# Turning batch 3's k with the transposing DMA in place of TensorE, and loading batch 4's k one slot sooner, in a sliding-window attention and MLP kernel

## The chip, the core and the metric

The kernel runs on one core of a Trainium2 chip. Its engines are TensorE (PE in the profile; PEld are its weight loads), VectorE (DVE), ScalarE (ACT), GpSimd (POOL) and SyncE (SP, which here does nothing but issue DMAs in order). Each engine works through its own queue in order and waits for the others by semaphores. The metric is the device time of one execution in microseconds.

## The reference

Attention with 8 batches, 8 heads, 576 positions and a head size of 64, in float32; a position sees itself and the 127 before it, and a bias that falls with the distance is added. The result, with the heads side by side, goes through a two-layer MLP with a hard-swish between the layers.

```python
scores = scale * np.matmul(q, k.transpose(0, 1, 3, 2))
bias = slopes[:, None, None] * (-np.abs(rel).astype(np.float32))[None, :, :]
mask = (rel >= 0) & (rel < window)              # window = 128
scores = np.where(mask, scores + bias[None], -1000000000.0)
attn = softmax(scores)                          # written out in the reference
attn_out = np.matmul(attn, v)
x = attn_out.transpose(0, 2, 1, 3).reshape(B * S, H * D)     # 4608 x 512
h = x @ w_in                                    # 512 -> 2048
g = h * np.clip(h + 3.0, 0.0, 6.0) / 6.0
out = g @ w_out                                 # 2048 -> 512
```

## The kernel before

The unit of attention is a pair of heads of one batch, numbered g = 4 x batch + pair, so g runs from 0 to 31. The MLP works on tiles of 512 tokens: 16 groups of matmuls up (`moe_up`, line 513) and 16 down (`moe_down`, line 539) per tile. `fill(n)` (line 574) issues the next n groups of that list, so that TensorE has MLP work between the steps of attention. The order of every queue is the order in which the program is written (`manual_schedule`); nothing reorders it.

From g = 8 on the work runs in `segment` (line 718), one slot per g. A slot has the scores of g (`scores`, lines 365 and 373), its exponentials on ACT (`exp_diag`, `exp_off`, lines 389, 413 and 418), which POOL masks (`affine_select`, lines 406, 415 and 421), and the product with v of the pair before (`values(g - 1, ...)`, lines 434 and 442), which VectorE divides by the row sums (lines 452 and 453). Groups of four MLP matmuls (lines 502 and 552) stand between these steps; an up group is followed by line 521 on ACT and line 522 on VectorE, and each finished block of 128 output rows is copied by VectorE (line 561) and stored by SP (line 562). `back` brings the attention result into the layout of the MLP: for most g by a transposing DMA on SP (line 476), for g = 10 and 11 by TensorE (line 483).

The scores need q and k with the head dimension on the partitions, in `qTb` and `kTb`, two buffers each that batches take in turn. Three ways lead there:

- `transposes`, for batch 0, and `prepare_double` (line 224) with `double` or `wide_double` for batches 1 and 2 and for batch 3's k: the load puts nine positions of each of four heads on one partition, POOL casts to bf16 (line 228), TensorE turns nine blocks of 128x128 (line 243) into PSUM, and ACT or VectorE copies them into `qTb` or `kTb` (line 245). One call of `double` does five or four of the nine blocks. It borrows the PSUM bank "av", which `values` also uses, or "h", which the up groups use.
- For batch 3's q and everything from batch 4 on: `load_tokens` (line 108, five DMAs of 256 KB and less on SP), POOL's cast into the one buffer `tbuf` (`cast_tokens`, line 195) and one transposing DMA of 20 blocks of 128x128 from `tbuf` into `qTb` or `kTb` (`xbar`, line 200). As there is one `tbuf`, POOL can't cast k before the transpose of q has landed.

`stage_next(g)` (line 591), near the end of each slot, issues the loads that the table `LOADS` (line 586) names for the slot, the casts and the transposing DMAs. The float32 loads share four buffers `ldbuf`; batch 4's k goes where batch 3's q was. At most eight DMAs of SP's have a semaphore each, taken in turn.

In the slots that matter here SP's queue reads: slot 9, loads of v3 and the transpose of q3; slot 10, a store, back(9), loads of q4; slots 11 and 12, three stores, loads of k4, the transpose of q4; slot 13, back(12), loads of v4, the transpose of k4. In slots 10 and 11 TensorE turns batch 3's k (`double(3, 0, "k", ...)` and `double(3, 1, "k", ...)`, first half after the scores, second half after the first group of the slot).

Of the kernel before, what the change touches and what calls it, by code (L numbers as in the profile page):

```python
# [11 lines left out]
BF16 = mybir.dt.bfloat16  # L12
# [6 lines left out]
def kernel(  # L19
# [9 lines left out]
    nc = tc.nc  # L29
# [6 lines left out]
    NP = H // 2  # L36
# [200 lines left out]
    def double(b, dp, nm, part, tag, copy):  # L237
        src = st[b, dp, nm]
        t0, t1 = ((0, 5), (5, RT))[part]
        tp = BANKS[tag].tile([128, t1 - t0, 128], BF16, tag=tag, name="tp2",  # L240
                             padded_shape=[128, 8, 128])
        for t in range(t0, t1):
            nc.tensor.transpose(tp[:, t - t0, :], src[:, t, :], ident)  # L243
        dst = (qTb if nm == "q" else kTb)[b % 2][:, 2 * dp:2 * dp + 2, :, :]
        copy(out=dst.rearrange("p i j c -> p i (j c)")[:, :, 0:S].rearrange(  # L245
                 "p i (a t) -> p i a t", t=RT)[:, :, :, t0:t1],
             in_=tp.rearrange("p t (a i) -> p i a t", i=2))

    def wide_double(b, dp, nm, copy):
# [324 lines left out]
    def fill(n):  # L574
        for _ in range(n):
# [3 lines left out]
            if fn is moe_up and done[0] < NP * (min((nt * NT + NT - 1) // S, B - 1) + 1):  # L579
# [3 lines left out]

    V, P, A = nc.vector.tensor_copy, nc.gpsimd.tensor_copy, nc.scalar.copy

    LOADS = {9: "v3", 10: "q4", 12: "k4", 13: "v4", 14: "q5", 16: "k5", 17: "v5", 18: "q6",
             20: "k6", 21: "v6", 22: "q7", 24: "k7", 25: "v7"}

    VCAST = {15: 4, 19: 5, 23: 6, 27: 7}
# [1 line left out]
    def stage_next(g):  # L591
        b, hp = divmod(g, NP)
        nb = b + 1
        if g == 2 * NP:
            cast_tokens(2, "v")
        for n in LOADS.get(g, "").split():
            load_tokens(int(n[1]), n[0])
        if nb == 3 and hp < 2:
            prepare_double(3, hp, (P,), "k")
        if nb == 3 and hp == 1:  # L600
            cast_tokens(3, "q")
            xbar(3, "q")
        elif nb < B and nb > 3 and hp < 2:
            cast_tokens(nb, "qk"[hp])
            xbar(nb, "qk"[hp])
        if VCAST.get(g):
            cast_tokens(VCAST[g], "v")
# [110 lines left out]
    def segment(lo, hi, fills):  # L718
        for g in range(lo, hi + 1):
            f = fills(g)  # L720
            if by_xbar(g - 2):
                done[0] = g - 1
            if lo < g < hi and g != 3 * NP + 1:
                scores(g)
            turn = {2 * NP: (2, 1, "k"), 2 * NP + 1: (2, 1, "q"),
                    2 * NP + 2: (3, 0, "k"), 2 * NP + 3: (3, 1, "k")}.get(g)
            if turn:
                double(*turn, 0, "av", A)
            fill(f[0])
            if turn:  # L730
                double(*turn, 1, *(("h", V) if turn[0] == 2 else ("av", A)))
            if g < hi:
                exp_diag(g, 0)
            fill(f[1])
            if g < hi:
                exp_diag(g, 1)
            if g == 3 * NP:
                cast_tokens(3, "v")
            if g > lo:
                values(g - 1, (0, 1, 2))  # L740
            fill(f[2])
            if g < hi:
                exp_off(g, 0)
            fill(f[3])
            if g < hi:
                exp_off(g, 1)
            if g > lo:
                values(g - 1, (3, 4))
            fill(f[4])
            if g > lo and by_xbar(g - 1):  # L750
                back(g - 1)
            fill(f[5])
            if g < hi:
                stage_next(g)
            fill(1)
            if g == 3 * NP:
                scores(g + 1)
            if g > lo and not by_xbar(g - 1):
                back(g - 1)
                done[0] = g  # L760
            fill(f[6] - 1)
# [51 lines left out]
```

## Time and profile before

| What | Value |
|---|---|
| median of 3 runs | 321.79 us (320.87 to 321.81) |
| profiled execution | 320.94 us, its span 319.2 us |
| granted TensorE clock | 0.999 |
| TensorE busy | 310.1 us (97%) |
| VectorE, ACT, POOL busy | 173.1, 195.7, 141.2 us |
| DMAs | 51.90 MB, 131425 packets |
| L243 transposes on TensorE (batches 2 and 3) | 45, 219 ns each |
| L245 copies on ACT, kTb | 0.73 to 0.77 us each |
| L476 transposing DMAs, 5 blocks | 22, hold SP 1.25 us (median), land in 2.7 |
| L200 transposing DMAs, 20 blocks | 9, hold SP 3.7 to 4.6 us, land 5.3 to 7.4 after issue |

A row of a timeline gives the start, the time taken, the engine, the line of the kernel, the operation and what it writes and reads; in brackets the engine's idle time before it and who ended that. For SP the time is how long the issue held the queue; the data land later. Matmuls are pipelined: four matmuls of 512 columns take 0.87 us from start to start, though the row says 1.03.

### The profile page before, as it was taken

How to read it: one execution, taken by the hardware profiler on the slowest of the kernel's cores; microseconds unless marked ns; L12 is line 12 of the kernel's file. 1: busy time of each engine (PE TensorE's matmuls, PEld its weight loads, DVE VectorE, ACT ScalarE, POOL GpSimd, SP SyncE). 2: the span in 40 equal slices, each digit the busy share in tenths (PEclk: the TensorE clock that was granted, in tenths of full speed). 3: DMA queues.
4: the chain of work that ended last, by engine and by line, in shares of the span. 5: the costliest groups of instructions: out<-in, count | busy, mean ns of one | idle time of the engine just before them, and what ended most of it. 6: DMA issues, size and time to landing. Idle time of an engine off the chain costs nothing.

```text
span 319.2 us, 7124 instructions
## 1 busy us (share of the span) xinstructions
PE 310.1 (97%) x2775; PEld 164.9 (52%) x2775; DVE 173.1 (54%) x338; ACT 195.7 (61%) x334; POOL 141.2 (44%) x249
## 2 busy tenths in 40 slices
PE   7879999999999999999999999999999999999996
PEld 5565465455545454445677654444444444444443
DVE  6667675554355655655565556555656455455510
ACT  4748976877767776676676667666764344244401
POOL 8464493684496477266744673663331000000000
PEclk9999999999999999999999999999999999999999
DMA  7999999999999999998999999962212110000112
GB/s 281 199 323 225 256 260 195 249 231 194 215 252 157 239 208 211 205 222 194 207 205 211 209 190 196 225 93 68 38 39 88 53 36 33 33 33 35 66 56 75
DMA packets 131425, 51.90 MB, mean 163 GB/s; under 512 B 118976, under 2 KB 123328, under 8 KB 131392
## 3 DMA queue, kind: packets, MB, share of 16 engines
q1 hardware_dynamic: 126160, 45.36, 68.0%
q0 software_dynamic: 4224, 4.19, 8.2%
q10 hardware_dynamic: 1008, 1.90, 1.6%
q8 instruction: 21, 0.34, 0.5%
q14 instruction: 12, 0.10, 0.1%
HBM read 36.70 MB, written 9.44 MB: 145 GB/s over the span
## 4 chain that ended last, share of the span: by engine, by line
PE 86%; DMA 5%; ACT 4%; POOL 2%; DVE 2%; issue 1%; POOLq 0%
PE ops L552 38%; PE hps L502 36%; DMA w_in_sb<-in_moe_w_in_dram 3%; PE sce L365 3%; PE av L442 2%; PE av L434 2%; DMA ldbuf<-in_k_dram 2%; ACT r L521 2%; PE ops L533 1%; ACT kTb L245 1%; ACT gbuf L399 1%; PE tp L243 1%; DVE gbuf L522 0%; ACT gbuf L377 0%; PE tb L483 0%
## 5 line engine op out<-in xcount | busy, mean ns | idle before, releaser
L522 DVE SCALAR_TENSOR_TENSOR gbuf<-r,hps 128x512 bf16<-128x512 f32 x144 | 98.7, 688 | 101.0 <-ACT r L521 99.8
L521 ACT ACTIVATE r<-hps,bias 128x512 f32<-128x512 f32 x144 | 98.9, 689 | 86.8 <-PE hps L502 86.6
L502 PE MATMUL hps<-xT,w_in_sb 128*128 128x512 bf16 (+1 forms) x640 | 144.9, 358 | 0.6 <-ACT xT L489 0.3
L552 PE MATMUL ops<-w_out_sb,gbuf 128*128 128x512 bf16 x560 | 137.8, 379 | 0.0
L502 PEld LDWEIGHTS <-w_in_sb 128*128 128x128 bf16 x640 | 59.3, 98 | 55.0 <-issue 0.8
L552 PEld LDWEIGHTS <-gbuf 128*128 128x128 bf16 x560 | 51.9, 98 | 56.3
L415 POOL TENSOR_SCALAR_AFFINE_SELECT po<-po 128x512 bf16<-128x512 bf16 x48 | 30.3, 636 | 32.5 <-ACT po L413 32.4
L406 POOL TENSOR_SCALAR_AFFINE_SELECT pd<-pd 128x512 bf16<-128x512 bf16 x48 | 29.8, 634 | 33.5 <-ACT pd L389 33.5
L389 ACT ACTIVATE pd<-sce,bias_d 128x512 bf16<-128x512 f32 x48 | 31.7, 684 | 5.4 <-PE sce L373 2.7
L561 DVE COPY osb<-ops 128x512 f32<-128x512 f32 x33 | 22.7, 688 | 20.0 <-PE ops L552 17.5
L195 POOL CAST tbuf<-ldbuf 128x512 bf16<-128x512 f32 (+1 forms) x45 | 25.6, 614 | 16.8 <-issue 9.3
L413 ACT ACTIVATE po<-sce,bias_o 128x512 bf16<-128x512 f32 x48 | 33.0, 687 | 0.0
L453 DVE TENSOR_TENSOR avs<-av,rc 128x384 bf16<-128x384 f32 (+1 forms) x48 | 23.6, 491 | 1.6
L442 PEld LDWEIGHTS <-pd 128*128 128x128 bf16 x192 | 14.3, 97 | 8.3 <-issue 0.5
L434 PE MATMUL av<-vbuf,po 128*128 128x65 bf16 x192 | 18.0, 193 | 0.0
L442 PE MATMUL av<-vbuf,pd 128*128 128x65 bf16 x192 | 17.3, 193 | 0.3 <-ACT kTb L245 0.3
L434 PEld LDWEIGHTS <-po 128*128 128x128 bf16 x192 | 14.3, 98 | 2.9 <-DVE avs L453 0.5
L188 POOL CAST vbuf<-ldbuf 128x1024 bf16<-128x1024 f32 x14 | 14.2, 1043 | 3.5 <-DMA ldbuf<-in_v_dram 3.5
L418 ACT ACTIVATE p4buf<-sce,bias_d 128x64 bf16<-128x64 f32 x48 | 15.5, 323 | 0.0
L228 POOL CAST pr<-ldbuf 128x576 bf16<-128x576 f32 x20 | 12.9, 670 | 5.1 <-DMA ldbuf<-in_k_dram 3.1
L365 PE MATMUL sce<-qTb,kTb 64*64 64x192 bf16 (+1 forms) x368 | 11.9, 245 | 0.0
L365 PEld LDWEIGHTS <-kTb 64*64 64x64 bf16 x368 | 7.1, 106 | 8.6 <-issue 8.5
(104 smaller groups left out, 208.4 us busy)
## 6 DMA issues: line engine op xcount, KB each, us to landing
out_dram<-osb SPq DMA_DIRECT2D x33, 256.0 KB, 2.5
ldbuf<-in_v_dram SPq DMA_DIRECT2D x32, 256.0 KB, 5.2
ldbuf<-in_q_dram SPq DMA_DIRECT2D x20, 256.0 KB, 5.3
ldbuf<-in_k_dram SPq DMA_DIRECT2D x16, 256.0 KB, 4.4
ldbuf<-in_q_dram SPq DMA_DIRECT2D x12, 288.0 KB, 7.0
ldbuf<-in_k_dram SPq DMA_DIRECT2D x12, 288.0 KB, 6.3
w_in_sb<-in_moe_w_in_dram POOLq DMA_DIRECT2D x4, 512.0 KB, 9.2
w_out_sb<-in_moe_w_out_dram POOLq DMA_DIRECT2D x4, 512.0 KB, 10.3
```

What stands on the lines that cost most here:

```text
L195: nc.gpsimd.tensor_copy(out=tbuf[:m, :, j, :], in_=s[:m, j, :, :].rearrange("p (i e) d -> p i (e d)", e=2))
L365: nc.tensor.matmul(sce[e][lo:lo + 64, j, :, :].rearrange("p s c -> p (s c)")[:, ds(lo, n)], lhsT=kT[r, j, lo:lo + 64], rhs=qT[r, ds(128 * ...
L389: nc.scalar.activation(out=pd[:, e, :, :], in_=st["sce"][e][:, :, 0, :], func=ACT.Exp, bias=bias_d[:, h:h + 1], scale=scale)
L406: nc.gpsimd.affine_select(out=pd[:, e, :, :], in_=pd[:, e, :, :], pattern=[[0, 4], [1, 128]], channel_multiplier=-1, base=0, compare_op=AL ...
L413: nc.scalar.activation(out=po[:, e, :, :], in_=sc[:, :, 1, :], func=ACT.Exp, bias=bias_o[:, h:h + 1], scale=scale)
L415: nc.gpsimd.affine_select(out=po[:, e, :, :], in_=po[:, e, :, :], pattern=[[0, 4], [-1, 128]], channel_multiplier=1, base=-1, compare_op=A ...
L434: nc.tensor.matmul(out_av, lhsT=po[:, e, qt % 4 if full(g) else qt - 1, :], rhs=vb[:, qt - 1, h, :], start=True, stop=False)
L442: nc.tensor.matmul(out_av, lhsT=d, rhs=vb[:, qt, h, :], start=(qt == 0), stop=True)
L502: nc.tensor.matmul(hps[:, lo:hi], lhsT=w_in_sb[:, ks, ts(ms, 128)], rhs=xT[:, ks, ds(src, hi - lo)], start=(ks == 0), stop=(ks == n_ks - 1))
L521: nc.scalar.activation(out=r6, in_=hps, func=ACT.Relu, bias=bias3[:, 0:1], scale=1.0 / 6.0)
L522: nc.vector.scalar_tensor_tensor(out=gts[nt][:, ms, :], in0=r6, scalar=1.0, in1=hps, op0=ALU.min, op1=ALU.mult)
L552: nc.tensor.matmul(ops[nt, sub], lhsT=gts[nt][:, ms, ts(sub, 128)], rhs=w_out_sb[:, ms, :], start=(ms == 0), stop=(ms == n_ms - 1))
```

## The change

Batch 3's k is no longer turned by `double` on TensorE. Once POOL has cast its halves into `pr` tiles (as before, in slots 8 and 9), a new function `turn_double` issues one transposing DMA of nine blocks on SP for each half, into a second SBUF tile: for the first half in slot 9, behind the loads of v3 and ahead of the transpose of q3, for the second in slot 10, behind the loads of q4. A second new function, `copy_double`, has VectorE copy each turned half into `kTb`, the first late in slot 11 (behind the second part of `values(10)`), the second in slot 13 (behind the first exponential). Four ACT copies out of PSUM go with the 18 transposes, and the "av" bank is no longer borrowed there. In `LOADS`, batch 4's k moves from slot 12 to slot 11, which on SP puts its five loads ahead of the store of slot 12.

```diff
+    def turn_double(b, dp, nm):
+        src = st.pop((b, dp, nm))
+        tp = st[b, dp, nm] = prs.tile([128, RT, 2 * D], BF16, tag="prq", name="pt2")
+        nc.sync.dma_start_transpose(out=tp, in_=src.rearrange("p t c -> p (t c)"))
+
+    def copy_double(b, dp, nm, copy):
+        tp = st.pop((b, dp, nm))
+        dst = (qTb if nm == "q" else kTb)[b % 2][:, 2 * dp:2 * dp + 2, :, :]
+        copy(out=dst.rearrange("p i j c -> p i (j c)")[:, :, 0:S].rearrange(
+                 "p i (a t) -> p i a t", t=RT),
+             in_=tp.rearrange("p t (a i) -> p i a t", i=2))
...
-    LOADS = {9: "v3", 10: "q4", 12: "k4", 13: "v4", 14: "q5", 16: "k5", 17: "v5", 18: "q6",
+    LOADS = {9: "v3", 10: "q4", 11: "k4", 13: "v4", 14: "q5", 16: "k5", 17: "v5", 18: "q6",
...
             load_tokens(int(n[1]), n[0])
+        if nb == 3 and hp in (1, 2):
+            turn_double(3, hp - 1, "k")
         if nb == 3 and hp < 2:
             prepare_double(3, hp, (P,), "k")
...
-            turn = {2 * NP: (2, 1, "k"), 2 * NP + 1: (2, 1, "q"),
-                    2 * NP + 2: (3, 0, "k"), 2 * NP + 3: (3, 1, "k")}.get(g)
+            turn = {2 * NP: (2, 1, "k"), 2 * NP + 1: (2, 1, "q")}.get(g)
             if turn:
                 double(*turn, 0, "av", A)
             fill(f[0])
             if turn:
-                double(*turn, 1, *(("h", V) if turn[0] == 2 else ("av", A)))
+                double(*turn, 1, "h", V)
             if g < hi:
                 exp_diag(g, 0)
+            if g == 3 * NP + 1:
+                copy_double(3, 1, "k", V)
...
             fill(f[4])
+            if g == 2 * NP + 3:
+                copy_double(3, 0, "k", V)
```

## The prediction

> **What bounds the kernel now.** I read the page first (shares, the chain that ended last), then the timelines of TensorE, of the SP queue and of POOL over 68 to 140 us. The page says that TensorE bounds the whole:
>
> ```profile
> span 319.2 us, 7124 instructions
> PE 310.1 (97%) x2775; PEld 164.9 (52%) x2775; DVE 173.1 (54%) x338; ACT 195.7 (61%) x334; POOL 141.2 (44%) x249
> DMA  7999999999999999998999999962212110000112
> PE 86%; DMA 5%; ACT 4%; POOL 2%; DVE 2%; issue 1%; POOLq 0%
> ```
>
> The reader should see two things: TensorE has about 9 us of idle time in all, and the DMA engines are as full as it is until about 208 us (26 slices of 8 us). So a microsecond taken from TensorE is worth one only if its data then also come a microsecond sooner. The timeline of TensorE in slot 10 shows what the change takes away:
>
> ```profile
> 68.80 0.52 PE L365 MATMUL sce<-qTb,kTb 64*64 64x192 bf16 x16
> 69.28 0.45 PE L243 MATMUL tp<-ident,pr 128*128 128x128 bf16 x5
> 69.56 1.03 PE L502 MATMUL hps<-xT,w_in_sb 128*128 128x512 bf16 x4
> 70.58 0.38 PE L243 MATMUL tp<-ident,pr 128*128 128x128 bf16 x4
> 70.80 1.03 PE L552 MATMUL ops<-w_out_sb,gbuf 128*128 128x512 bf16 x4
> 71.99 0.22 PE L442 MATMUL av<-vbuf,pd 128*128 128x65 bf16 x2 [0.17 <-ACT kTb L245]
> ```
>
> The timeline of the SP queue shows what it adds to (second column: how long the issue held the queue):
>
> ```profile
> 70.46 5.51 SPq L112 DMA_DIRECT2D ldbuf<-in_v_dram  x5
> 76.08 3.81 SPq L200 DMA_TRANSPOSE qTb<-tbuf  x1
> 80.40 0.38 SPq L562 DMA_DIRECT2D out_dram<-osb  x1
> 80.88 1.26 SPq L476 DMA_TRANSPOSE xT<-avs  x1
> 82.20 4.50 SPq L112 DMA_DIRECT2D ldbuf<-in_q_dram  x5
> ...
> 89.67 0.33 SPq L562 DMA_DIRECT2D out_dram<-osb  x1
> 90.06 4.50 SPq L112 DMA_DIRECT2D ldbuf<-in_k_dram  x5
> 94.77 3.85 SPq L200 DMA_TRANSPOSE qTb<-tbuf  x1
> ...
> 105.82 3.83 SPq L200 DMA_TRANSPOSE kTb<-tbuf  x1
> ...
> 125.83 3.75 SPq L200 DMA_TRANSPOSE qTb<-tbuf  x1
> ```
>
> Each row begins about 0.1 us after the one before it ends (0.5 once, at 80.40). Between 76 and 126 us the only real pause is 1.8 us ahead of 89.67 (the wait list: that store waited for VectorE). The queue is full. And its transposes end at TensorE, as POOL's and TensorE's timelines show:
>
> ```profile
> 133.43 2.84 POOL L195 CAST tbuf<-ldbuf 128x512 bf16<-128x512 f32 x5 [5.73 <-DMA qTb<-tbuf]
> 137.41 1.22 POOL L415 TENSOR_SCALAR_AFFINE_SELECT po<-po 128x512 bf16<-128x512 bf16 x2
> 138.82 0.23 PE L442 MATMUL av<-vbuf,pd 128*128 128x65 bf16 x2
> ```
>
> **What is removed.** 18 transposes, 4 ACT copies (0.73 to 0.76 us each) and their hand-over of the av bank. Slot 10 (scores at 68.80 to scores at 76.94) lasts 8.14 us and slot 14 (98.16 to 105.33), with the same scores, values and seven groups of four MLP matmuls, 7.17: 0.97 us for nine transposes. Slot 11 (76.94 to 85.37) lasts 8.43, of which back(10) takes 0.38: 8.05 against 7.17, 0.88 us. TensorE gains 0.97 + 0.88 = 1.85 us. The ACT copies lie beside other work and give nothing more.
>
> **What is added on SP.** Two transposes of nine blocks, which the trace lacks. Five blocks (L476) hold the queue 1.25 us and twenty (L200) 3.81: 0.17 per block and 0.4 fixed, so 1.94 us for nine, 2.04 with the usual 0.1 gap. Ends: 1.25 and 3.85. I take 1.94, as the two rows span it. Landing: twenty blocks land 5.3 to 7.4 us after issue, and 2.1 us behind the load ahead of them (k4's last landed 4.5 after 93.47, the transpose of q4 5.3 after 94.77): 0.105 per block, so nine land about 1 us behind what is in flight.
>
> The Trainium skill (DMA: Bandwidth & Descriptors, "Issuing engines are not separate DMA queues") says that the sequencer's time to start a DMA is usually small beside the DMA. This trace disagrees: 3.81 of 5.4 us. By the rule the queue would hardly slip, and the sum would be that of the second rival. The skill also speaks against the change: VectorE: DVE Perf Modes, "The three transpose paths", puts a 128x128 transpose at 390 ns on TensorE and 1309 ns by DMA, and nine of those would be 11.8 us. By it the turn of k3 high, issued at 88.4, would land at 100 and the sum would be some +6 us. The trace disagrees here too: twenty blocks land in 5.4 us.
>
> **What moves on SP.** In the new order the queue runs: v3 loads, turn of k3 low, transpose of q3, store, back(9), q4 loads, turn of k3 high, two stores, k4 loads, the store that paused, transpose of q4. Nothing else changes place. k4's source buffer is free (q3 was cast by 72.3 us), so its loads fill the 1.8 us pause. Step by step, from 76.08:
>
> - transpose of q3: 78.1 instead of 76.08. It landed 5.4 us after issue, so at 83.5 instead of 81.5.
> - q4 loads 83.8 instead of 82.20; turn of k3 high at 88.4; k4 loads from 91.6, about 1.5 later than before in spite of the earlier slot.
> - transpose of q4: two turns of 2.04, less 1.7 of the pause, 0.1 of a wait for POOL's cast ahead of 94.77, and 0.4 more if the gap at 80.40 is chance: 1.8 to 2.2, so I take 2.0 us later, 96.8. Transpose of k4 107.8 instead of 105.82, as back(12) and v4 between them keep their lengths. The queue has no pause over 0.2 us before 125.83 to win the 2.0 back. With the ends above (1.25, 3.85) the slip is 0.6 or 5.8.
>
> **What is added on VectorE.** Two copies of 128x1152 out of SBUF. Nearest rows: the same shape out of PSUM, L257, 1.35 us; half the elements from SBUF, L182, 0.56. I take 1.35, the same pattern; ends 0.56 and 1.36. The first stands after avs of values(10), which ends 1.85 sooner than 84.1 (L453, 83.69 + 0.42), so 82.3 to 83.6; the store's copy of rows behind it (L561, 84.33) has time, its bank is next written at 92.3. The scores of slot 12, now due at 85.37 - 1.85 = 83.5, need this copy (83.6) and q3 (83.5): TensorE loses about 0.2. The second copy waits for its turn: q4's last load, issued at 85.55, landed 5.1 later, 90.6, and now 92.3, plus 1: 93.3, while VectorE is there at about 92.2. Queued behind it are reciprocal and product of values(12), which free the av bank: 93.3 + 1.35 + 0.19 + 0.56 = 95.4, and the second half of values(12), at 96.10 before, starts 0.65 sooner. Of 1.85 us 0.65 are left here, and the cost is gone again at the next points, which are set by landings.
>
> **Where TensorE meets the queue.**
> - Slot 16's scores (112.50) need the transpose of k4, which landed 5.4 us after 105.82, at 111.2: spare 1.25. With 2.0 of slip TensorE stands 0.75 behind the kernel before.
> - The masks ahead of values(14): POOL's cast of k4 waited for q4's transpose and started at 100.27; its po masks ended at 105.5, values(14) ran at 107.55: spare 2.1, just enough.
> - The masks ahead of values(18): POOL's cast of k5 waited until 133.43 (q5's transpose, landed 7.4 after 125.83); the second po mask ended at 138.6 and its matmul ran at about 138.9: spare 0.3. With 2.0 of slip TensorE stands 1.7 behind. If that transpose took the median 6.0 of the nine, not 7.4, only 0.3, and slot 16's 0.75 stays.
> - Later spares are larger: 2.2 at slot 20's scores, 1.8 at values(22), 0.9 at values(26).
>
> These are not added: each puts TensorE where its data are, and the largest counts. After 208 us the DMA engines are idle, TensorE alone sets the pace, and what it is behind stays. The sum lies between +0.75 and +1.7; the transpose keeps its neighbours in the queue, with which it took 7.4, so I stay nearer that end: +1.3. Against the profiled execution, 320.94 us (span 319.2 and 1.74 around it), that is 322.2. The median of the runs shown, 321.79, lies 0.85 above it: **323.1 us**.
>
> **Rivals.** A measurement of this kernel tells about 0.3%, 1 us, from no change.
>
> 1. The slip is partly taken back. A load holds the queue 0.57 us when it is unhindered and about 1.0 when the DMA engines are behind; a turn gives them time, so the loads behind it could issue faster. For: 0.4 us times two or three loads. Against: after the long transposes, which give them still more time, load blocks of five take 4.4 to 5.7 all the same. Slip 0.5 to 1.1, less 0.3 or, where q5's transpose lands in 6.0, less 1.25: -0.75 to +0.8 us, 321.0 to 322.6.
> 2. Faster. If a nine-block turn holds SP no longer than an unhindered load, 0.57, the slip is 2 x 0.67 less some 2.0 (the pause and half of the uncertain gap) = -0.6: the k4 move wins. Then values(18) is the tightest point, at -0.6 - 0.3 = -0.9, and the full -1.85 is had if q5's transpose lands in 6.0. 319.9 to 320.9. It decides where a turn holds SP less than about 1.1 us, which makes the slip the 0.3 that values(18) has to spare. For: the pause filled is real. Against: five blocks already hold it 1.25.
> 3. The turn costs more than its blocks: held as long as a twenty-block one, or landing 7.4 us after issue, with the VectorE copy of slot 13 waiting and the MLP products queued behind it. Slip 3 to 5.8, less the spare of 0.3 to 1.25: +2.5 to +4.5, 324.3 to 326.3. Against: the two rows give a straight line.
>
> **How the numbers follow.** Forecast 0.48 (its own range 322.5 to 323.6), rival one 0.18, two 0.17, three 0.17. Faster by over 0.3% (below 320.8): most of rival two, 0.15. Slower (above 322.8): most of the forecast, 0.38, and rival three, 0.17: 0.55. Within: the rest, 0.30. The range 320.6 to 324.8 leaves out about half of rival two and over half of rival three, under 0.2. Forecast and rivals of the other sign are both likely, so the forecast's own range stands beside it.
>
> **What would show it.** Right: slots 10 and 11 about 0.9 us shorter each; two transposes of about 1.9 us on SP; those of q4 and k4 issued about 2 us later; an idle of TensorE at slot 16's scores waiting for kTb, or at values(18) waiting for POOL, that is not there before. Wrong: turns under 1 us on SP, or the transpose of k4 issued no later than 105.8, would make it faster; a stall of several us at VectorE's copy in slot 13 would make it slower than the range.

## The result, and the profile after

| | before | after |
|---|---|---|
| median of 11 runs | 322.13 us (320.87 to 324.00) | 324.55 us (322.69 to 326.15) |
| ratio after / before | | 1.0078, 95% interval 1.0053 to 1.0103 |
| profiled execution, its span | 320.94 us, 319.2 us | 325.48 us, 323.8 us |
| granted TensorE clock in it | 0.999 | 0.994 |

The change made the kernel 0.8% slower: 2.4 us in the medians, 4.6 us between the two profiled executions. The page of after, its first lines and the granted clock (40 slices of 8.1 us):

```profile
span 323.8 us, 7052 instructions
PE 307.7 (95%) x2718; PEld 164.7 (51%) x2757; DVE 175.6 (54%) x340; ACT 193.2 (60%) x330; POOL 141.1 (44%) x249
...
PEclk9999999999999899999999999999999999999999
DMA  7999999999999999999899999962011201000112
```

TensorE is busy 2.4 us less than before, and the span is 4.6 us longer: what was taken from TensorE came back as idle time. (Part of the 2.4 is not saved: the page of after lists 622 matmuls at L514 and 539 at L564 where the page of before has 640 and 560, so some are missing from the trace.) The digit 8 in the fourteenth slice of PEclk is new, and the DMA engines are as full as they were. In the kernel after, lines below the two new functions are 12 higher than the same lines before (L365 is L377, L502 is L514); lines above them, such as L112, L195 and L200, keep their numbers.

Where the time went is read from the starts of the slots, that is of their first scores in the timeline of TensorE. The kernels start slot 9 up to 2.7 us apart though their code is the same up to there, so all starts are set equal at slot 9, here and wherever a time is said to be against slot 9. The account is of one profiled execution of each kernel. That of before is a short one (320.94 us; the median is 322.13) and that of after a long one (325.48; 324.55), which is why its +4.33 us is more than the 2.4 us of the medians. Minus is sooner than before:

| Kernel (experiments below) | slot 12 | slot 14 | slot 16 | slot 18 |
|---|---|---|---|---|
| after | -1.09 | +0.19 | +4.33 | +4.33 |
| a1_k4_back | -1.06 | +1.41 | +3.06 | +3.06 |
| a2_k4_alone | -0.02 | -0.02 | -0.03 | -0.03 |
| a3_turns_aside | +0.01 | +0.01 | +3.86 | +3.86 |
| a4_no_turn | -1.92 | -0.93 | -0.93 | -0.93 |
| b1_copy_late | -1.90 | -0.45 | +4.42 | +4.42 |
| b2_two_buffers | -1.16 | +0.40 | +1.45 | +1.60 |
| b3_q4_loads_aside | +9.22 | +10.96 | +10.97 | +10.97 |
| b4_all_three | +9.13 | +13.39 | +13.39 | +13.39 |
| c1_v4_behind | -1.52 | 0.00 | 0.00 | +2.69 |
| c2_turn_first | -1.52 | -1.52 | +5.67 | +5.66 |
| c3_order | -1.91 | -1.91 | -1.91 | +4.02 |
| c4_loads_on_act | 0.00 | 0.00 | +0.86 | +0.86 |

Kernels whose code is the same up to slot 12 differ there by up to 0.8 us (after -1.09, b1_copy_late -1.90), so a single entry is no surer than that.

In the kernel after, slot 10 lasts 7.17 us in place of 8.14 and slot 11, without the wait at its end, 7.52 in place of 8.43: the 1.88 us that TensorE was to gain. They go in three places, at the ends of slots 11, 13 and 15. TensorE's timeline of after; in brackets its idle time and what ended it:

```profile
84.70 0.52 PE L377 MATMUL sce<-qTb,kTb 64*64 64x192 bf16 x16 [0.80 <-ACT xT L501]
...
96.69 0.20 PE L446 MATMUL av<-vbuf,po 128*128 128x65 bf16 x1 [1.10 <-DVE avs L465]
...
108.95 0.20 PE L454 MATMUL av<-vbuf,pd 128*128 128x65 bf16 x1 [0.64 <-POOL pd L418]
109.54 0.20 PE L454 MATMUL av<-vbuf,pd 128*128 128x65 bf16 x1 [0.38 <-POOL pd L418]
110.13 0.20 PE L446 MATMUL av<-vbuf,po 128*128 128x65 bf16 x1 [0.38 <-POOL po L427]
...
110.71 0.20 PE L446 MATMUL av<-vbuf,po 128*128 128x65 bf16 x1 [0.35 <-POOL po L427]
...
110.90 1.38 PE L564 MATMUL ops<-w_out_sb,gbuf 128*128 128x512 bf16 x4
112.07 3.27 PE L514 MATMUL hps<-xT,w_in_sb 128*128 128x512 bf16 x8
```

Slot 12's scores wait 0.80 us (the named ACT had long been done; the transpose of q3 landed at 84.56). Slot 13 lasts 10.16 in place of 8.88 us, 1.28 more, with a wait of 1.10 for VectorE, whose second copy waits for its turn and holds up the normalisation (L464, L465) queued behind it:

```profile
94.42 1.52 DVE L257 COPY kTb<-pt 128x1152 bf16<-128x1152 bf16 x1 [1.14 <-DMA pt<-pr]
```

In values(14), which run in slot 15, each of the four masks is waited for as POOL makes it. Then eight matmuls that usually take 1.9 us take 3.27. The timelines of the SP queue and of POOL show why the masks are late:

```profile
75.51 3.66 SPq L252 DMA_TRANSPOSE pt<-pr  x1
79.68 3.14 SPq L200 DMA_TRANSPOSE qTb<-tbuf  x1
...
89.03 1.79 SPq L252 DMA_TRANSPOSE pt<-pr  x1
...
92.84 4.71 SPq L112 DMA_DIRECT2D ldbuf<-in_k_dram  x5
...
98.50 3.69 SPq L200 DMA_TRANSPOSE qTb<-tbuf  x1
...
108.91 3.76 SPq L200 DMA_TRANSPOSE kTb<-tbuf  x1
```

```profile
94.23 2.20 POOL L418 TENSOR_SCALAR_AFFINE_SELECT pd<-pd 128x512 bf16<-128x512 bf16 x2
...
105.48 2.83 POOL L195 CAST tbuf<-ldbuf 128x512 bf16<-128x512 f32 x5 [7.63 <-issue]
108.27 1.21 POOL L418 TENSOR_SCALAR_AFFINE_SELECT pd<-pd 128x512 bf16<-128x512 bf16 x2
109.44 1.22 POOL L427 TENSOR_SCALAR_AFFINE_SELECT po<-po 128x512 bf16<-128x512 bf16 x2
```

q4's transpose goes out at 98.50 in place of 94.77 and lands at 105.37 in place of 100.12. POOL stands still for 7.63 us: its next work is the cast of k4 into `tbuf`, the tile that this transpose is still reading. The cast runs from 105.48 (before: 100.27), the masks of slot 14 stand behind it in POOL's order, and TensorE meets them one by one.

What the granted clock does there is in the view by windows; the last three columns are PEclk, the DMA share and GB/s:

```profile
108.30:111.40 3.10, 1.34 (x14) 0.76 (x14) 0.95 (x3) 2.05 (x4) 3.10 (x7) 1.00 1.50 204
111.40:114.80 3.40, 3.40 (x10) 1.25 (x9) 1.24 (x3) 0.69 (x1) 1.26 (x3) 0.51 0.99 244
114.80:117.20 2.40, 2.40 (x19) 1.02 (x16) 1.70 (x4) 1.47 (x3) 0.48 (x1) 0.99 0.72 163
```

After 3.1 us in which TensorE worked for 1.34, its granted clock is half (0.51 in the view) for 3.4 us, which costs 1.7. Slot 15 lasts 11.30 us in place of 7.17: of the 4.13, 1.75 are the four waits, 1.7 the clock, and the rest the single matmuls between the masks. The sum of the slots is -0.97 - 0.91 + 0.80 + 1.28 + 4.13 = +4.33 us, and it stays to slot 18 and beyond. Of the eleven runs of after, six have a granted clock of 0.994 or 0.995 (median 325.3 us) and five 0.999 or 1.0 (median 323.8): without the half clock the change is still some 1.6 us slower than before.

### The profile page after: what moved, and what is told of

Its sections match the earlier page's. It is cut to its first block, busy times and chain, and to the rows that moved or that the text cites. A ratio compares the mean times of both kernels' runs of the same rounds, so it can differ in the third digit from the quotient of the medians.

```text
span 323.8 us, 7052 instructions
## 1 busy us (share of the span) xinstructions
PE 307.7 (95%) x2718; PEld 164.7 (51%) x2757; DVE 175.6 (54%) x340; ACT 193.2 (60%) x330; POOL 141.1 (44%) x249
## 4 chain that ended last, share of the span: by engine, by line
PE 82%; DMA 6%; ACT 4%; SPq 3%; DVE 2%; issue 2%; POOL 1%; ACTq 0%
PE ops L564 36%; PE hps L514 35%; PE sce L377 3%; DMA ldbuf<-in_q_dram 2%; PE av L454 2%; SPq L112 2%; PE av L446 2%; DMA pt<-pr 2%; DMA ldbuf<-in_k_dram 2%; ACT r L533 1%; PE ops L545 1%; DVE gbuf L534 1%; SPq L98 1%; ACT gbuf L411 1%; ACT xT L501 1%
## 5 line engine op out<-in xcount | busy, mean ns | idle before, releaser
L514 PE MATMUL hps<-xT,w_in_sb 128*128 128x512 bf16 (+1 forms) x622 | 144.2, 360 | 1.9 <-DMA w_in_sb<-in_moe_w_in_dram 0.4
L564 PE MATMUL ops<-w_out_sb,gbuf 128*128 128x512 bf16 x539 | 134.2, 380 | 2.6 <-issue 2.1
L514 PEld LDWEIGHTS <-w_in_sb 128*128 128x128 bf16 x640 | 59.6, 98 | 57.1 <-issue 2.9
L564 PEld LDWEIGHTS <-gbuf 128*128 128x128 bf16 x560 | 51.9, 98 | 56.7 <-issue 0.3
L418 POOL TENSOR_SCALAR_AFFINE_SELECT pd<-pd 128x512 bf16<-128x512 bf16 x48 | 30.5, 651 | 31.4 <-ACT pd L401 31.4
L195 POOL CAST tbuf<-ldbuf 128x512 bf16<-128x512 f32 (+1 forms) x45 | 25.7, 611 | 22.1 <-issue 21.5
L465 DVE TENSOR_TENSOR avs<-av,rc 128x384 bf16<-128x384 f32 (+1 forms) x48 | 23.6, 491 | 1.6
L377 PE MATMUL sce<-qTb,kTb 64*64 64x192 bf16 (+1 forms) x368 | 11.9, 245 | 0.8 <-ACT xT L501 0.8
L377 PEld LDWEIGHTS <-kTb 64*64 64x64 bf16 x368 | 7.2, 106 | 9.5 <-issue 8.5
```

Source lines behind the costliest of these rows:

```text
L195: nc.gpsimd.tensor_copy(out=tbuf[:m, :, j, :], in_=s[:m, j, :, :].rearrange("p (i e) d -> p i (e d)", e=2))
L377: nc.tensor.matmul(sce[e][lo:lo + 64, j, :, :].rearrange("p s c -> p (s c)")[:, ds(lo, n)], lhsT=kT[r, j, lo:lo + 64], rhs=qT[r, ds(128 * ...
L418: nc.gpsimd.affine_select(out=pd[:, e, :, :], in_=pd[:, e, :, :], pattern=[[0, 4], [1, 128]], channel_multiplier=-1, base=0, compare_op=AL ...
L514: nc.tensor.matmul(hps[:, lo:hi], lhsT=w_in_sb[:, ks, ts(ms, 128)], rhs=xT[:, ks, ds(src, hi - lo)], start=(ks == 0), stop=(ks == n_ks - 1))
L564: nc.tensor.matmul(ops[nt, sub], lhsT=gts[nt][:, ms, ts(sub, 128)], rhs=w_out_sb[:, ms, :], start=(ms == 0), stop=(ms == n_ms - 1))
```

## The experiments

Each was compared with the kernel before in the same stretch of chip time (its median was 321.6 to 321.9 us). Two questions stood first: is it the move of k4's loads, the DMAs or the VectorE copies, and is it SP's time?

**k4's loads back in their slot.** The change without its second half.

```diff
-    LOADS = {9: "v3", 10: "q4", 11: "k4", 13: "v4", ...
+    LOADS = {9: "v3", 10: "q4", 12: "k4", 13: "v4", ...
```

> The changed kernel with batch 4's k loaded in slot 12 again. Queue theory (the two turns make SP late, so the transpose of q4 and with it POOL's masks come late): the pause ahead of slot 12's store is gone once SP is late, so there is nothing for the earlier slot to fill; ratio to the kernel before 1.005 to 1.011, as the changed kernel. Rival (the moved load does the harm): 0.994 to 1.000.

Measured: 324.25 us, ratio 1.0084 (1.0057 to 1.0111). Against slot 9, q4's transpose went out 0.45 us and landed 0.42 us later than with the move: nearly the same. The profiled execution has a longer wait in slot 13 (2.30 us) and no half clock.

**k4's loads alone.** The kernel before with only that line changed.

```diff
-    LOADS = {9: "v3", 10: "q4", 12: "k4", 13: "v4", ...
+    LOADS = {9: "v3", 10: "q4", 11: "k4", 13: "v4", ...
```

> The kernel before with only batch 4's k loaded in slot 11. Queue theory: the pause of 1.8 us is filled, but the transpose of q4 was issued 0.2 us after POOL's cast of q4 ended and can't come sooner, so ratio 0.998 to 1.002. Rival (the moved load does the harm): above 1.005.

Measured: 322.71 us, ratio 1.0021 (0.9993 to 1.0048), no slot changed by more than 0.03 us. The move neither gains nor costs anything that can be measured, with the turns or without. Against slot 9 the first of the loads went out and the last landed 0.9 us sooner, but q4's transpose had to wait for POOL's cast and went out at 94.85, as before (94.77). One thing here matters for what follows (SP's row for that transpose, and POOL's for the cast behind it):

```profile
96.01 4.27 SPq L200 DMA_TRANSPOSE qTb<-tbuf  x1
```

```profile
103.44 2.83 POOL L195 CAST tbuf<-ldbuf 128x512 bf16<-128x512 f32 x5 [3.80 <-DMA qTb<-tbuf]
```

With no turn in the kernel, this transpose landed 7.3 us after its issue where it had taken 5.3 before, 2.0 us later against slot 9. TensorE did not wait for it: values(14) had just that much to spare.

**The turns alone.** The kernel before, its TensorE transposes kept, with k4's loads in slot 11 and the two DMAs into a tile that nothing reads.

```diff
+    def turn_aside(b, dp, nm):
+        tp = prs.tile([128, RT, 2 * D], BF16, tag="prq", name="pt2")
+        nc.sync.dma_start_transpose(out=tp, in_=st[b, dp, nm].rearrange("p t c -> p (t c)"))
...
-    LOADS = {9: "v3", 10: "q4", 12: "k4", 13: "v4", ...
+    LOADS = {9: "v3", 10: "q4", 11: "k4", 13: "v4", ...
...
+        if nb == 3 and hp in (1, 2):
+            turn_aside(3, hp - 1, "k")
```

> The kernel before, TensorE's 18 transposes and their copies kept, with k4 in slot 11 and with the two nine-block transposing DMAs issued at their places in the changed kernel into a tile that nothing reads. Queue theory: TensorE's place is set by landings, so the loss is that of the changed kernel or up to 1 us less, ratio 1.004 to 1.011. Rival (VectorE's copy in slot 13, which waits for its turn, does the harm): no such copy here, 0.998 to 1.002.

Measured: 325.37 us, ratio 1.0116 (1.0097 to 1.0136), just over what the theory gave. The turns held SP 1.82 and 1.65 us, q4's transpose went out at 98.47 and landed at 105.13. TensorE's timeline:

```profile
108.72 0.20 PE L446 MATMUL av<-vbuf,pd 128*128 128x65 bf16 x1 [0.36 <-POOL pd L410]
109.31 0.20 PE L446 MATMUL av<-vbuf,pd 128*128 128x65 bf16 x1 [0.38 <-POOL pd L410]
109.89 0.20 PE L438 MATMUL av<-vbuf,po 128*128 128x65 bf16 x1 [0.38 <-POOL po L419]
110.48 0.20 PE L438 MATMUL av<-vbuf,po 128*128 128x65 bf16 x1 [0.35 <-POOL po L419]
```

The same four waits at values(14), and +3.86 us at slot 16: the two DMAs do this on their own. TensorE's gain and the VectorE copies have no part in it.

**The copies alone.** The change without its two DMAs: VectorE copies what POOL had cast, and batch 3's k stays unturned.

```diff
     def turn_double(b, dp, nm):
-        src = st.pop((b, dp, nm))
-        tp = st[b, dp, nm] = prs.tile([128, RT, 2 * D], BF16, tag="prq", name="pt2")
-        nc.sync.dma_start_transpose(out=tp, in_=src.rearrange("p t c -> p (t c)"))
+        pass
```

> The changed kernel without the two transposing DMAs: VectorE copies the cast, unturned tile into kTb (batch 3's scores are therefore those of a k in the wrong layout). Queue theory: TensorE's 1.85 us are gained as far as landings let it, the transposes of q4 and k4 are issued no later than before, ratio 0.994 to 0.999. Rival (VectorE's copies themselves cost, by holding up the values): 1.002 or more.

Measured: 321.86 us, ratio 1.0003 (0.9981 to 1.0025). That lies between what the theory and the rival gave, and the medians show no gain. Against slot 9 the transposes of q4 and k4 go out 0.4 and 0.9 us sooner than before, as the theory said. By the slots the kernel gains 1.92 us up to slot 12 and loses 0.99 of it in slot 13, where TensorE waits 0.82 us for the normalisation behind the second copy. VectorE's row for that copy, and the one of c3_order below:

```profile
93.66 2.47 DVE L255 COPY kTb<-pr 128x1152 bf16<-128x1152 bf16 x1
```

```profile
92.38 1.44 DVE L258 COPY kTb<-pt 128x1152 bf16<-128x1152 bf16 x1
```

Here the copy runs beside two of POOL's masks, which take 2.14 us for 1.22. In c2_turn_first and c3_order the masks come after it, as POOL's cast of q4 waits for its loads there, and slot 13 loses nothing. So the 0.99 us are not the price of the copy itself but of its meeting the masks.

**The second copy behind the fill.** The change, with `copy_double(3, 1, ...)` moved behind the second half of values(12).

```diff
-            if g == 3 * NP + 1:
-                copy_double(3, 1, "k", V)
             fill(f[1])
...
             fill(f[4])
+            if g == 3 * NP + 1:
+                copy_double(3, 1, "k", V)
```

> The change, with VectorE's second copy (slot 13) moved behind the fill of slot 13's second half, so that values(12) of that slot no longer wait for a normalisation queued behind the copy. In the changed kernel's trace that wait cost 1.10 us (slot 13's values on a tile of VectorE). Theory of the chain (what sets the time is the landing of q4's transpose, 5.25 us late, then GpSimd's cast of k4 into the same buffer, then the masks of values(14)): slot 13 comes 1.1 us sooner, but slot 14 waits that much longer for the masks, slot 16 begins where it did, +4.5 to +4.8 us against the kernel before, and the time is unchanged: 324.3 to 324.9, 1.006 to 1.010 of before. Rival (the copies on VectorE are a loss of their own, which lasts to the end): 1.1 us of it come back, 323.2 to 323.8, 1.003 to 1.006.

Measured: 326.84 us, ratio 1.0143 (1.0086 to 1.0200). The wait for the normalisation is gone, but slot 14's scores now wait 1.39 us for the copy itself, and the first mask of values(14) is waited for 1.58 us. Slot 16 begins at +4.42, as with the change: what is saved ahead of values(14) is lost there. The time of the runs was not what that theory said (324.3 to 324.9): all four had a granted clock of 0.990 to 0.995, against six of eleven with the change. That is a reason for some of the 2 us; the rest isn't explained.

**Two buffers for the casts.** The cast of k4 no longer waits for q4's transpose.

```diff
-    tbuf = held.tile([128, NP, NQ, 128], BF16, name="tbuf")
+    tbufs = {nm: held.tile([128, NP, NQ, 128], BF16, name=f"tbuf{nm}") for nm in "qk"}
...
-            nc.gpsimd.tensor_copy(out=tbuf[:m, :, j, :],
+            nc.gpsimd.tensor_copy(out=tbufs[nm][:m, :, j, :],
...
-                                    in_=tbuf.rearrange("p h j c -> p (h j c)"))
+                                    in_=tbufs[nm].rearrange("p h j c -> p (h j c)"))
```

> The change, with one GpSimd buffer for the cast q and a second one for the cast k in the place of one for both, so that the cast of k4 need not wait until q4's transpose has landed. Theory of the chain through that buffer: the cast of k4 begins when its load has landed and GpSimd is free, some 5 us sooner (about 100 instead of 105.5), the masks of values(14) are in time, the sparse matmuls of 108.3 to 110.9 and the half clock after them are gone (1.6 us and 1.7 us); what then binds is the landing of k4's transpose at slot 16, which stands behind q4's on SP. It landed at 114.1 in the changed kernel; the issue of q4's holds SP until about 102.3 and k4's could go right behind it, at 102.5 in the place of 108.9, landing about 108 to 110, ahead of slot 16 at 111. Time 321.4 to 322.6, 0.998 to 1.003 of before. Rival (SP's time itself sets the transposes, the buffer has no part): k4's transpose still lands at 113 to 114 and the time stays at 324 or over, 1.006 or more.

Measured: 324.41 us, ratio 1.0093 (1.0061 to 1.0125). The list of TensorE's waits from 70 to 125 us:

```profile
PE av L447 <- DVE avs L466: 1.4, 1, 1.4
PE sce L378 <- DMA kTb<-tbufk: 1.0, 1, 1.0
PE sce L378 <- ACT xT L502: 0.7, 1, 0.7
```

No mask is waited for and the half clock is gone from the profiled execution, so the chain through `tbuf` was real. But k4's transpose did not go out at 102.5, as I had said, but at 109.55, and landed at 114.81; slot 16's scores wait for it. Ahead of it on SP stood back(12) and five loads of v4. The rival had named that time and, to within 0.8 us, that landing. Half of the ten runs had the half clock after all, at 0.995.

**q4's loads from GpSimd's queue.** The bytes stay, SP is relieved of about 4 us.

```diff
-            nc.sync.dma_start(out=t[:n, j, :, :],
+            eng = nc.gpsimd if (b, nm) == (4, "q") else nc.sync
+            eng.dma_start(out=t[:n, j, :, :],
```

> The change, with q4's five loads issued by GpSimd instead of SP, the bytes and the turns as they are. Theory (SP's time is what slips: the turns hold it 3.66 and 1.79 us): SP is relieved of the five loads' 4.1 us between the turns, q4's transpose goes out within 1 us of 94.8, where it stood before the change (98.5 with it), values(14) wait for no mask, no half clock; the time is 321.2 to 322.6, 0.998 to 1.003 of before. Rival (it is the DMA engines that are full: the turns' blocks land behind the other transposes' and loads): q4's transpose goes out sooner but still lands at 104 to 105, values(14) still wait, and the time is 324 or over. A third: GpSimd's own issue time (five by about 0.8 us) delays its masks in slot 10 to 12 and a new wait on GpSimd appears there, 322.5 to 324.

Measured: 333.47 us, ratio 1.0322 (1.0247 to 1.0398), worse than any expectation. The SP queue, and one row of POOL's timeline:

```profile
77.38 3.70 SPq L253 DMA_TRANSPOSE pt<-pr  x1
81.58 9.03 SPq L201 DMA_TRANSPOSE qTb<-tbuf  x1
...
91.39 4.06 SPq L489 DMA_TRANSPOSE xT<-avs  x1
```

```profile
78.72 4.26 POOL L113 DMA_DIRECT2D ldbuf<-in_q_dram  x5
```

GpSimd gets to the loads at 78.72, where SP had come to them at 84.83, so they run beside the turn and the transpose. The transpose of q3 holds SP 9.03 us in place of 3.14 and lands 15.3 us after issue in place of 4.9; slot 12's scores wait 11.1 us for it. SP's own load fell, and its holds grew: how long a DMA holds SP is not its own cost alone but depends on what else the DMA engines have in hand. That SP's order had let the urgent transpose go first is one reading. It has a rival that was not tested: loads issued by GpSimd go through another kind of queue, which the profile calls software_dynamic, in packets of 3.2 KB (368 for 1.18 MB) where nearly all others are under 512 B, and from 78 to 97 us the engines moved only 147 GB/s, against 206 in the kernel after. A single load from ScalarE's queue (the last experiment) did no such harm.

**All three edits.**

```diff
+    (the edits of b1_copy_late, b2_two_buffers and b3_q4_loads_aside)
```

> The change with all three edits: the copy behind the fill, two buffers for the casts, q4's loads issued by GpSimd. If each removes what its theory names, nothing of slot 14 to 16 is left, and the gains of slots 10 and 11 (0.98 and 0.9) stay, less 0.5 to 0.8 that the first copy costs at slot 12: 320.4 to 321.4, 0.995 to 0.999 of before. If a wait of its own stands behind these (the masks of GpSimd, delayed by the five issues, or a copy that still holds a normalisation), 321.4 to 322.6.

Measured: 336.34 us, ratio 1.0435 (1.0365 to 1.0505). Slot 12's scores wait 11.0 us for the transpose of q3, as in the run before; the third edit hides what the others do.

**v4's loads behind k4's transpose**, with the two buffers.

```diff
-    LOADS = {..., 11: "k4", 13: "v4", 14: "q5", 16: "k5", ...
+    LOADS = {..., 11: "k4", 14: "v4 q5", 16: "k5", ...
```

> The change with two buffers for the casts, and v4's five loads moved from slot 13 to slot 14, behind k4's transpose on SP. With two buffers alone the masks of values(14) were in time, but k4's transpose went out at 109.55 and landed at 114.81 for scores at slot 16, which waited 1.0 us for it; v4's loads stood ahead of it from 104.41 to 109.45. Theory (the transposes are late because SP's queue and the DMA engines behind it have no free time, so only the order decides what is late): k4's transpose goes out about 5 us sooner, at 104.5, lands at 109 to 110, the wait at slot 16 is gone, and the time is 1.0 us under that of two buffers alone: slot 16 begins 0.3 to 0.6 us behind the kernel before when both are set equal at slot 9, 322.3 to 323.4, 1.002 to 1.005 of before. Rival (the masks or v4's cast are late next): a new wait in slots 16 or 17 takes the microsecond back, 324 or over.

Measured: 325.22 us, ratio 1.0093 (1.0061 to 1.0125). k4's transpose went out at 104.01 and landed at 109.54; slot 16 begins where it did before the change (0.00 in the table; +1.45 with the two buffers alone, of which 0.36 were there at slot 12 already). Then SP's queue and TensorE's timeline go on:

```profile
109.64 4.28 SPq L112 DMA_DIRECT2D ldbuf<-in_v_dram  x5
113.96 6.67 SPq L112 DMA_DIRECT2D ldbuf<-in_q_dram  x5
...
121.39 1.29 SPq L489 DMA_TRANSPOSE xT<-avs  x1
...
123.41 1.23 SPq L489 DMA_TRANSPOSE xT<-avs  x1
```

```profile
124.76 0.38 PE L515 MATMUL hps<-xT,w_in_sb 128*128 128x512 bf16 x1 [0.71 <-DMA xT<-avs]
126.79 1.24 PE L515 MATMUL hps<-xT,w_in_sb 128*128 128x512 bf16 x5 [1.66 <-DMA xT<-avs]
```

With ten loads in a row the small transposes of `xT` are late, and slot 17 gives 2.7 us away. The theory was right that the wait at slot 16 goes; on the time the rival was right, though the new wait is for `xT` and not, as it had said, for masks or v4's cast.

**The turns ahead of their slots' loads.** The change with two statements exchanged.

```diff
+        if nb == 3 and hp in (1, 2):
+            turn_double(3, hp - 1, "k")
         for n in LOADS.get(g, "").split():
             load_tokens(int(n[1]), n[0])
-        if nb == 3 and hp in (1, 2):
-            turn_double(3, hp - 1, "k")
```

> The change with each turn issued ahead of its slot's loads (v3's, q4's) instead of behind them; all else as it is. Theory (SP and the DMA engines are full; a turn costs q4's transpose the same wherever ahead of it it stands): the turns land 5 us sooner, the second VectorE copy no longer waits for its turn (1.14 us in the changed kernel), slot 13 loses 0.4 to 0.8 us in place of 1.28, but q4's transpose still goes out at about 98.5 and lands at about 105, values(14) still get their masks one at a time, slot 16 begins at the same +4.3 us (both set equal at slot 9), and the time is unchanged: 324.0 to 325.0, 1.006 to 1.010. Rival (the turns hold SP long only where they stand behind a full queue, 3.66 us for the first): their hold falls to 1.7 us, q4's transpose comes 1 to 2 us sooner and the time is 322.5 to 323.8.

Measured: 326.09 us, ratio 1.0128 (1.0081 to 1.0176). The turns held SP 1.49 and 1.31 us, so the rival was right that 3.66 was no price of a turn. But the loads behind them held it longer (five of v3 5.72 us for 4.60, five of q4 6.02 for 4.10), q4's transpose went out at 99.02 and landed at 105.74: what the turns no longer wait for, the loads do. Five loads and their turn together held SP 7.2 and 7.3 us in the two slots, and 8.3 and 5.9 in the kernel after: no less in all. Slot 13 lost nothing (-1.52 at slots 12 and 14), and values(14) gave all of it away and more: the first mask was waited for 2.55 us, and the half clock lasted 6.8 us (110.1 to 116.9). The time is 1 us over the theory's range.

**The order put right for one batch**: two buffers, v4's loads behind k4's transpose, turns ahead of the loads.

```diff
+    (the edits of b2_two_buffers, c1_v4_behind and c2_turn_first)
```

> Two buffers for the casts, v4's loads behind k4's transpose, and the turns ahead of their slots' loads, together. If each does what its theory says: no wait for masks, none for k4's transpose, 0.4 to 0.8 us left of the second copy and 0 to 0.7 of the first: slot 16 begins 0.3 to 1.0 us sooner than in the kernel before (both set equal at slot 9), 320.9 to 322.2, 0.997 to 1.001. If the copies on VectorE go on holding normalisations, 322.2 to 323.2.

Measured: 325.78 us, ratio 1.0128 (1.0084 to 1.0172). Ahead of slot 17 nothing waits: slot 16 begins 1.91 us sooner than before, the whole gain on TensorE, where I had expected 0.3 to 1.0. Then TensorE's timeline has the waits of c1_v4_behind again:

```profile
124.56 0.38 PE L515 MATMUL hps<-xT,w_in_sb 128*128 128x512 bf16 x1 [1.73 <-DMA xT<-avs]
126.46 2.20 PE L515 MATMUL hps<-xT,w_in_sb 128*128 128x512 bf16 x5 [1.52 <-DMA xT<-avs]
```

and the clock is half from 126.6 to 130.0. Slot 18 begins at +4.02. The expected time failed with it.

**The same load on the DMA engines, none on SP.** The kernel before with one more load of 256 KB in each of the two slots, from ScalarE's queue, into a tile that nothing reads. These loads go out at 67.76 and 74.81 us, sooner than the turns of the kernel after (75.51 and 89.03).

```diff
+    xld = held.tile([128, 4, H, D], FP32, name="xld")
...
+        if nb == 3 and hp in (1, 2):
+            for j in (hp,):
+                nc.scalar.dma_start(out=xld[:, j, :, :],
+                                    in_=v[7, :, ds(j * 128, 128), :].rearrange("h p d -> p h d"))
```

> The kernel before, with no turn and nothing of the change, but with one more load of 256 KB in slot 9 and one in slot 10, issued by ScalarE into a tile that nothing reads. A load of that size lands about 1.2 us behind the one before it, a turn about 0.94 to 1.1 behind the load before it, so the DMA engines carry about as much as with the two turns, and SP nothing. Theory of the engines: q4's transpose lands 2 to 4 us later than the 100.12 of before (relative to slot 9), and k4's 2 to 3 later than 111.25. Theory of SP's time: it goes out and lands within 0.7 us of where it did. The time is 321.8 to 322.8 by the first, 321.6 to 322.2 by the second; what is read is the landings.

Measured: 323.52 us, ratio 1.0064 (1.0032 to 1.0096), more than either theory had said. On SP, with no turn in it:

```profile
90.25 5.56 SPq L113 DMA_DIRECT2D ldbuf<-in_k_dram  x5
95.99 3.88 SPq L201 DMA_TRANSPOSE qTb<-tbuf  x1
...
106.17 3.84 SPq L201 DMA_TRANSPOSE kTb<-tbuf  x1
```

Against slot 9, q4's transpose goes out 1.5 us later and lands 3.05 later (102.89). The landing is within what the theory of the engines gave (2 to 4), but it does not tell the two theories apart: 1.5 us of it is a longer flight (6.9 us), and with k4's loads alone, where no load was added, the flight was 7.3. What does is the going out: 1.5 us later here, against 0.08 later with k4's loads alone and 0.37 sooner with the copies alone, where the theory of SP's time gave under 0.7. k4's transpose landed only 0.7 later, where 2 to 3 were expected: by then the lag had been made up. values(14) wait for two masks, 0.16 and 0.35 us. So in this execution load on the engines alone, with nothing added to SP's program, made SP late: its three blocks of five loads ahead of q4's transpose held it 2.9 us longer than before. How much of the turns' own delay, 3.3 us at the going out, is SP's time and how much the engines' isn't split by this, as the extra loads ran earlier than the turns.

The Trainium skill (DMA: Bandwidth & Descriptors, "Issuing engines are not separate DMA queues") says that DMAs started by different engines end up on the same 16 DMA engines and interleave. These two runs agree as far as they go: q3's transpose landed after 15.3 us beside loads from GpSimd's queue, and q4's went out 1.5 us later after loads from ScalarE's.

## Why the prediction came out as it did

The sign and the range were right (slower; 324.55 us against 323.1 predicted, in 320.6 to 324.8). The forecast's own range, 322.5 to 323.6, didn't hold the time. The kind of chain it named is what happened (the turns make SP late, a transpose lands late, TensorE waits), but at another place, values(14), and at the size of rival three. That the range held is in part luck: the time lies 0.25 us under its upper end, and the range took in a gain as well as a loss. In the profiled executions the forecast gave +1.3 us and +4.33 came; in the medians +2.4.

- **TensorE's gain, 0.97 + 0.88:** right, 0.97 + 0.91 in the kernel after, 1.92 with the copies alone, 1.91 in c3_order.
- **The slip of q4's transpose, 2.0 us on SP:** this is the step that failed. I added up what the turns would hold SP (1.94 each) and took 1.7 off for the pause that k4's loads fill. Against slot 9, q3's transpose went out 3.18 us later and q4's 3.31 (said: 2.0 for each), k4's 2.67. So the miss stands at the first turn, held 3.66 us, near the upper end of 3.85 that I had named. From there to q4's transpose hardly anything was added: the second turn (1.79) was balanced by shorter holds of others and by the pause, which a late SP no longer has. The move of k4's loads gave at most 0.45 us of that, by the run with the loads back in slot 12. The hold of a turn was no constant (1.27 to 3.70 us in the experiments), and where both turns were held short, 1.49 and 1.31 in c2_turn_first and 1.27 and 1.30 in c3_order, q4's transpose still went out 3.7 and 2.6 us later than before, as the loads behind the turns were held longer. So no sum of the turns' own holds gives the slip. By the view of windows the DMA engines' share is 0.92 or more in every slot from 9 to 15, in both kernels. (The share adds up the times of packets, which overlap, so that it reaches 1.33; it doesn't say that nothing more would fit.) I had said of the engines that they were as full as TensorE, and then made the sum on SP alone.
- **"It landed 5.4 us after issue":** it took 6.9, so that the landing slipped by 4.83 us against slot 9. The DMA view of after from 98 to 106 us, in slices of 0.2 us:

```profile
DMA  9999999999999999999999999992999000071449
GB/s 220 213 219 221 220 212 223 208 219 223 275 238 195 369 392 249 292 291 289 292 289 288 292 291 289 292 235 69 251 265 59 5 10 9 10 141 30 101 102 223
```

From 104.0 to 105.0 (the 31st to 35th slice) 5 to 59 GB/s move where it was 290, in the middle of the transpose. The kernel before has such a hole too, in slices of 0.25 us from 94:

```profile
GB/s 210 238 244 238 220 232 227 220 207 202 201 142 123 176 62 217 290 289 291 293 287 290 195 18 251 238 8 0 0 3 8 9 23 102 105 46 207 252 264 274
```

There it begins at 100.5, just behind the landing at 100.12. So the 1.5 us that the transpose takes longer to land go with a hole of about 1 us that it had just escaped before. What makes the holes wasn't tried. This part needs no turn: a2_k4_alone had it without one (7.3 us). The 5.3 of before was a short flight: of the eleven other kernels that leave q4's loads on SP, ten took 6.7 to 7.4. A delay of 2.0 us from this alone was what values(14) could bear; the 3.3 of the going out came on top.
- **The first VectorE copy, 0.2 us at slot 12:** 0.80. q3's transpose landed at 84.14 against slot 9 and not at 83.5, by the same mis-sized slip. How much TensorE waits there is not settled by the order: with the turns ahead of the loads it was 0.36 us (c2_turn_first) and nothing (c3_order), with the turns behind them from 0.83 (a1_k4_back) over 0.37 (c1_v4_behind) to nothing (b1_copy_late).
- **The second copy leaves 0.65 us:** not quite; slot 13 took 1.28 us, and 0.19 more than the whole gain was gone at slot 14. The copy began at 94.00 against slot 9 (said: 93.3) and took 1.52 us (1.35).
- **Where TensorE meets the queue:** the wrong point. values(14) had been given a spare of 2.1, "just enough" for a slip of 2.0. That was well read: in a2_k4_alone a landing 2.0 later cost nothing. With a landing 4.83 later it binds, and it binds before slot 16 does. Slot 16 with +0.75 and values(18) with +1.7 did not bind in the kernel after. With the buffers doubled slot 16 was the next (+1.45).
- **The half clock** wasn't foreseen; it is 1.7 of the 4.33 us.
- **Rival two, the faster one,** decided where a turn holds SP less than 1.1 us. It never did: the shortest was 1.27, and in c2_turn_first, with 1.49 and 1.31, the loads behind took the difference. **Rival one** fell with the same numbers: behind the turns q4's loads issued 0.40 us faster, but k4's 0.21 slower. **Rival three** was right in its size and in VectorE's copy of slot 13, and half right in its reason: the first turn was held nearly as long as a twenty-block one, but that was no price of a turn. With two buffers, at the same place, it was held 1.63 us, and the last two loads ahead of it 3.52, against 2.1 in the kernel after.

What stays open: which order would keep the gain. c3_order carries all of it to slot 16 and loses it to the `xT` transposes behind ten loads. How the turns' delay divides between SP and the DMA engines, and what the holes are, is not known either. An order with v4's loads in the empty slot 15 and its cast a slot later was not run.

## What to carry to other kernels

In these runs the time that an issue held the queue depended on what stood around it, so it was a symptom and not a price; before a DMA takes over work from another engine, ask for the DMA engines' share in that stretch. Here, where the share was near or over one throughout, a new DMA delayed the transfers behind it, a load moved ahead gained nothing that could be measured, and a reordering only picked which consumer waits; look for the one with the least spare, in both kinds of unit (a landing, and an engine's queue that a landing blocks). Take the flight of a DMA from several executions: one gave 5.3 us where most gave about 7. A few short waits of a bounding TensorE can cost twice, once as idle time and once as half clock.

## What the runs showed of the hardware

- **Half clock after little work, without a long pause.** In the kernel after no idle time of TensorE in slot 15 was over 0.64 us, and yet the clock was half for 3.4 us after 3.1 us in which TensorE worked for 1.34 (43%). In a1_k4_back, with three of the four waits, it worked 2.28 of 3.40 us (67%) from 109.0 to 112.4, and the clock stayed full. But it also stayed full in c1_v4_behind, where TensorE worked 1.13 of 3.50 us from 123.6 to 127.1, so the share alone does not decide. The half clock lasted 3.4 us here and in c3_order, 6.8 in c2_turn_first and 10.2 in b3_q4_loads_aside (of which the windows are below). The Trainium skill (TensorE: Matmul & The Clock Gate, "What's actually happening") gives a free-running window of 3413 ns, and those durations agree with one, two and three of it. Its rule of no idle gaps over about 3.4 us ("HAM oscillation", same page) does not cover a halving with gaps of 0.64 us. Where the limit lies, the runs don't show.

```profile
85.00:90.50 5.50, 0.94 (x9) 0.46 (x6) 1.69 (x2) 0.64 (x1) 0.62 (x2) 1.00 1.17 157
90.50:100.70 10.20, 3.65 (x27) 1.74 (x28) 0.31 (x1) 2.64 (x6) 1.89 (x3) 0.50 1.07 208
100.70:102.00 1.30, 1.30 (x16) 0.70 (x14) 0.45 (x2) 0.19 (x1) 1.30 (x3) 0.99 1.32 265
```

- **A VectorE copy from SBUF and POOL's masks slow each other.** Two masks that otherwise take 1.22 us took 2.20 beside the second copy (POOL's row at 94.23 above), and the copy 1.52 where the first had taken 1.25. In a4_no_turn the masks took 2.14 and the copy 2.47, where the first had taken 1.30.
- **The hold of one and the same transposing DMA on SP** went from 3.04 to 9.03 us for twenty blocks and from 1.27 to 3.70 for nine: 1.27 to 1.72 with no loads right ahead of it on SP, 1.63 to 3.70 behind five loads.
- **The flight of a twenty-block transpose varies without any DMA added.** q4's, issued at the same point, landed 5.3 us after issue before and 7.3 with k4's loads moved by 0.9 us.
